# Two layers of memory-segment attention and ReLU blocks: banks of five and three turned slots, moved input moments and mask, an ordered ReLU, memory tokens by VectorE

## The chip, the core and the metric

The kernel runs on one core of a Trainium2 chip. TensorE (PE) multiplies, VectorE (DVE) and ScalarE (ACT) read its results out of PSUM and do the elementwise work, GpSimd (POOL) does elementwise work in SBUF, and SyncE (SP) issues most of the DMAs. The metric is the time of one execution on the device, in microseconds (us); 1589.74 is the median of three runs of the kernel before.

## The reference

Two identical layers; a layer is a recurrent attention over segments and a ReLU block, each behind a layer norm and added to its input (x has 2048 rows of 512).

```python
def _A_ref(x, mem0, Wq, Wk, Wv, Wo, seg_len):     # H=32, Dh=128, M=8, seg_len=32
    mask = (idx[:, None] < M) | (idx[:, None] >= idx[None, :])
    mem = mem0
    for s in range(n_seg):                        # 64 segments, one after the other
        h = jnp.concatenate([mem, xs], axis=1)    # 8 memory tokens and 32 rows
        q, k, v = (einsum('btd,dhe->bhte', h, W) for W in (Wq, Wk, Wv))
        scores = jnp.where(mask, (q @ k.T) * scale, -1e9)
        p = _softmax(scores, axis=-1)
        o = einsum('bhte,hed->btd', p @ v, Wo)
        mem = o[:, :M, :]                         # the next segment's memory
        outs.append(o[:, M:, :])
def _B_ref(x, w1, w2):                            # Dff=1376
    return maximum(x @ w1, 0) @ w2
x = x + _A_ref(_layernorm(x), ...); x = x + _B_ref(_layernorm(x), ...)   # twice
```

The memory of segment s comes out of segment s-1, so that the 64 segments of a layer are a chain.

## The kernel before

The kernel walks through 68 steps k = 0 to 67. A step handles segment k of the first layer (a = 0) and segment k-4 of the second (a = 1), each where it exists, so that steps 4 to 63 have both ("dual" here) and the first four and last four have one ("single"). L = 40 tokens a segment; tokens of both layers lie side by side in HT as 80 columns, so one weight load of Wq or Wk serves both.

A dual step, in TensorE's order: half 0 of the heads (queries and keys in batches of 6, 6 and 4 heads, `qk`, L592, matmuls on L578), a piece of the deferred output projection of the step before (`block`, L364), scores of half 0 (L612), queries and keys of half 1, the dense block's first product (`dense_h`, L495), scores of half 1, more of the output projection, the dense block's second product (`dense_y`, L520, first 18 matmuls of it), the transposes of half 1's probabilities (`transpose_p`, L652), the last 4 matmuls of `dense_y`, the weighted values (`weighted_v`, L670, matmuls on L685), the memory tokens' output (`output_mem`, L616), values of the second layer (`values1`), the turning of the new memory (`new_memory`, L817, tile mt), and the memory's values (`memory_values`, L759, matmuls on L768). Then the next step's queries begin.

Who does what beside that:

- Query results are evicted from PSUM by ScalarE (L584), key results by VectorE (L586). They share the pool ps_c of three banks, so the third query batch takes the bank of the first key batch. ps_c also holds the tiles that probabilities are turned through, mt and the memory's values.
- The score banks `sp_tiles` are filled with the mask by VectorE (`masks`, L602) before the scores are added into them. For half 0 this is done in `normalize_step` at the end of the step before; for half 1 inside `qk(1, ...)`, one mask behind the second key eviction and one behind the third.
- Softmax: maximum (L628) and subtraction (L632) on VectorE, exponential on ScalarE (L634), sum and reciprocal on VectorE (L644, L645), multiplication (L649) on POOL, but on VectorE for the last layer of half 1. Half 0's probabilities are turned by a transposing DMA (`turn_p`, L666). Half 1's are turned by TensorE in two PSUM tiles of four slots (a slot is two heads), one evicted by ScalarE and one by VectorE (L663).
- The dense block's first product is evicted with a ReLU by ScalarE (L518), in two pieces.
- `new_memory` writes the new memory tokens from mt into HT (for queries and keys, VectorE, L841) and into HTm (for the memory's values, ScalarE, L838).
- Input rows come in blocks of 128. A block is loaded (`load_xb`, at k%4 = 0), gets its moments (`moments_x`, L230) in step k%4 = 1, is normalized (L227) at the end of step k%4 = 2, and is turned by a transposing DMA (`inputs_T`) in step k%4 = 3. There are blocks to do for k = 2 and for dual steps up to k = 47.
- In k = 5, 9, ..., 49 the values of three further groups of input heads are computed (`values_at`, `split`). These steps are called light here, after the name in the code; in them `dense_h` is emitted in two pieces, the second behind half 1's scores and softmax, and ScalarE copies the values to vst (L311).

The queues of PE, DVE, SP and POOL take the instructions in the order in which the program emits them (`manual_schedule`); ScalarE's order is made by the framework's planner. `high_priority` marks blocks for that planner. `tc.issue_after(ins)` puts the instructions of its block behind `ins` on their engine.

Of the kernel before, what the change touches and what calls it, by code (L numbers as in the profile page):

```python
# [8 lines left out]
F32 = mybir.dt.float32  # L9
ALU = mybir.AluOpType  # L10
ACTF = mybir.ActivationFunctionType
# [11 lines left out]
def kernel(  # L23
# [14 lines left out]
    nc = tc.nc  # L38
    _, S, Dm = A_x.shape
    _, H, Dh = A_Wq.shape[0], A_Wq.shape[1], A_Wq.shape[2]  # L40
    M = A_mem0.shape[1]
# [3 lines left out]
    L = M + SEG  # L45
# [7 lines left out]
    SCALE = float(Dh) ** -0.5  # L53
# [6 lines left out]
    ps_c = ctx.enter_context(tc.tile_pool(name="ps_c", bufs=3, space=PSUM))  # L60
# [41 lines left out]
    xbs = {}  # L102
# [84 lines left out]
    HT = const.tile([128, NC4, 2, L], BF)  # L187
# [8 lines left out]
    P_sb = const.tile([128, 8, 128], BF)  # L196
    nc.gpsimd.memset(P_sb[:], 0.0)
    P1_sb = const.tile([128, 16 * L + 24], BF)
    nc.gpsimd.memset(P1_sb[:], 0.0)
    PT_sb = const.tile([128, 8, 2, L], BF)  # L200
    PT0 = const.tile([128, 8, 128], BF)
# [15 lines left out]
    def stat_tail(stats, of=""):  # L217
        mom = wk.tile([128, 3], F32, tag="ln_mv" + of, bufs=2 - len(of), name="mv")
        mv, rstd = mom[:, 0:2], mom[:, 2:3]
        nc.vector.bn_aggr(out=mv, in_=stats[:])  # L220
        nc.vector.tensor_scalar_add(out=rstd, in0=mv[:, 1:2], scalar1=LN_EPS)  # L221
        nc.gpsimd.tensor_tensor(out=rstd, in0=rstd, in1=mhalf_t[:], op=ALU.pow)  # L222
        return mv, rstd

    def normalize(eng, dst, src, mom, lo, hi):
        mv, rstd = mom
        eng.tensor_scalar(out=dst[lo:hi, :], in0=src[lo:hi, :], scalar1=mv[lo:hi, 0:1], scalar2=rstd[lo:hi, 0:1],  # L227
                          op0=ALU.subtract, op1=ALU.mult)

    def moments_x(n):  # L230
        stats = wk.tile([128, 6], F32, tag="ln_stats", bufs=1)
        nc.vector.bn_stats(out=stats[:], in_=xbs[n][:])
        return stat_tail(stats, "x")

    def transpose_pe(xn):
        tp = ps_fill.tile([128, NC4, 128], BF, tag="fill", name="tpx")
# [255 lines left out]

    def dense_h(d, parts=slice(None)):  # L495
        if not 0 <= d <= LAST:
            return
        lo, hi = span(d)
        n = hi - lo

        def cols(c4):
            return xnT_tiles[d + 2][:, c4, lo:hi]

        if not parts.start:
            hT_tiles[d] = wk.tile([128, NFC, 64], BF, tag="hT", bufs=1, name="hT")
        hT = hT_tiles[d]
        pieces = ((8, NFC), (0, 4), (4, 8)) if d == LAST - 1 else ((8, NFC), (0, 8))
        for f0, f1 in pieces[parts]:
            hp = ps_fill.tile([128, 8, 64], F32, tag="fill", name="hp")
            for fc in range(f0, f1):  # L510
                u = F_LAST + 128 * fc if fc < NFC - 1 else 0
                for c4 in range(NC4):
                    nc.tensor.matmul(hp[:, fc - f0, 0:n], lhsT=w1_sb[:, c4, u:u + 128],  # L513
                                     rhs=cols(c4), start=(c4 == 0), stop=(c4 == NC4 - 1))
            if (f0, f1) == (4, 8):
                nc.vector.tensor_scalar_max(out=hT[:, f0:f1, 0:n], in0=hp[:, 0:f1 - f0, 0:n], scalar1=0.0)
            else:
                nc.scalar.activation(out=hT[:, f0:f1, 0:n], in_=hp[:, 0:f1 - f0, 0:n], func=ACTF.Relu)  # L518

# [72 lines left out]
    def qk(hf, act, between=None, behind=None):  # L592
        res = []
        for n, (o, nh) in enumerate(BATCHES):
            res.append((o, nh) + tuple(qk_batch(n, 16 * hf + o, nh, act[0], act[-1] + 1, None if n else between)))
            if n == 0 and behind:
                behind()
            if hf and n > 0:
                masks(*act[n - 1:n])
        return res  # L600

    def masks(*act):  # L602
        for a in act:
            nc.vector.tensor_copy(out=sp_tiles[a], in_=maskb2)  # L604
# [11 lines left out]
    def output_mem(k, wo, h0=0, h1=H):  # L616
        n, c = divmod(k % 4, 2)
        for h in range(h0, h1):
            j = h % 4
            nc.tensor.matmul(wo[32 * j:32 * j + 32, :], lhsT=OTm[:, h, n, 2 * M * c:2 * M * c + 4 * M], rhs=Wo_sb[:, h, :],  # L620
                             start=(h < 4), stop=(h >= H - 4), tile_position=(0, 32 * j))

    def exponentials(act):
        mxs, ess = {}, {}
        for a in act:
            sp = sp_tiles[a]
            mxs[a] = wk.tile([128, 8], F32, tag="mx", bufs=2, name="mx")
            nc.vector.tensor_reduce(out=mxs[a][:], in_=sp, axis=AX.X, op=ALU.max)  # L628
        for a in act:
            sp = sp_tiles[a]  # L630
            es = ess[a] = wk.tile([128, 8, L], F32, tag="es", bufs=2, name="es")
            nc.vector.tensor_tensor(out=es[:], in0=sp, in1=mxs[a][:].unsqueeze(2).to_broadcast([128, 8, L]),  # L632
                                    op=ALU.subtract)
            nc.scalar.activation(out=es[:], in_=es[:], func=ACTF.Exp, scale=SCALE)  # L634
        return ess

    def softmax(hf, act, by_pe=False, ess=None):
# [11 lines left out]
            eng.tensor_tensor(out=P, in0=es[:],  # L649
                              in1=sm[:].unsqueeze(2).to_broadcast([128, 8, L]), op=ALU.mult)  # L650

    def transpose_p(hf):  # L652
        for p, copy in ((0, nc.scalar.copy), (1, nc.vector.tensor_copy)):
            tp = ps_c.tile([128, 4, 2, L], F32, tag="c", name="tp")
            for sl in range(4):
                for a in range(2):
                    c = L * (2 * (4 * p + sl) + a)
                    P = P1_sb[:, c:c + 64] if hf else P_sb[:, 4 * p + sl, 64 * a:64 * a + 64]
                    nc.tensor.matmul(tp[64 * a:64 * a + 64, sl], lhsT=P, rhs=ident_q,  # L659
                                     start=True, stop=True, tile_position=(0, 64 * a))  # L660
            PT = PT_sb[:, 4 * p:4 * p + 4] if hf else \
                PT0[:, 4 * p:4 * p + 4].rearrange("p s (g q) -> p s g q", g=2)[:, :, :, 0:L]
            copy(out=PT, in_=tp[:])  # L663

    def turn_p():
# [151 lines left out]
    def new_memory(k, cont, wo):  # L817
        wm_sb = wm_tiles[k] = wk.tile([128, Dm], BF, tag="vst", bufs=5, name="wm")
        nc.scalar.copy(out=wm_sb[:], in_=wo[:])
        values1(k + 1, 0)  # L820
        if k == 2:
            values0(*values_at(k)[0])
        c = 1 - k % 2
        mt = ps_c.tile([128, NC4, 2, M], F32, tag="c", name="mt")
        for c4 in range(NC4):
            for r in range(0, 128, 32):
                nc.tensor.matmul(mt[r:r + 32, c4].rearrange("p a m -> p (a m)"),  # L827
                                 lhsT=wm_sb[:, c4 * 128 + r:c4 * 128 + r + 32],
                                 rhs=sel[:, 4 * M * c:4 * M * c + 2 * M], start=True, stop=True,
                                 tile_position=(0, r))  # L830
        lo, hi = cont[0], cont[-1] + 1

        single = len(layers(k)) == 1
        by_act = k == 0 or has1(k + 1)

        def to_values():
            copy = nc.scalar.copy if by_act else nc.vector.tensor_copy
            copy(out=HTm[:, :, lo * M:hi * M], in_=mt[:, :, lo:hi, :].rearrange("p c a m -> p c (a m)"))  # L838

        def to_queries():  # L840
            nc.vector.tensor_copy(out=HT[:, :, lo:hi, 0:M], in_=mt[:, :, lo:hi, :])  # L841

        for f in (to_values, to_queries) if single else (to_queries, to_values):
            f()

    def prepare(k):
        if k <= LAST:
# [54 lines left out]
    def step(k):  # L902
        act = layers(k)
        single = len(act) == 1
        cont = [a for a in act if k - DELTA * a + 1 < NSEG]
        n_x = k // 4 + 4
        has_x = n_x < NXT
# [4 lines left out]
        with tc.high_priority(offset=PRIO):  # L912
            behind = norm_rows.pop(k, None)
            if k == 1:
                def behind():
                    normalize(nc.vector, xbs[3], xbs[3], moments_x(3), 0, 128)
            qks = qk(0, act, behind=behind)
            load_values(k, act)
            if k == 1:
                memory_values(k)  # L920
                inputs_T(3)
# [5 lines left out]
        with tc.high_priority(offset=PRIO):  # L927
            transpose_step(k)
            load_memory_values(k, act)
            scores(qks, act)  # L930
            ess = exponentials(act)

        def probabilities():

# [22 lines left out]
        if single:  # L957
            dense_h(k - 2, slice(0, 1) if k == LAST else slice(None))
            block(k, mid, H)
            if k == LAST:  # L960
                keep_busy(3)
        elif light:
            dense_h(k - 2, slice(1, None))
            block(k, 16, H)
        else:
            block(k, part, H)
# [4 lines left out]
            add_output(k - 1)  # L971
        if k == LAST:
            add_last(k - 1, 0)
        if (k % 4 == 1 and k > 1 or k == 2) and has_x:
            mom["x"] = moments_x(n_x)
        with tc.high_priority(offset=PRIO):
            transpose_p(1)
        if ahead and k < LAST:
            dense_y(k - 2, f_mid, NFC)
        tokens_in(k + 1)  # L980
# [35 lines left out]
                memory_values(k + 1)  # L1016
        with tc.high_priority(offset=PRIO):
            prepare(k + 1)
        if k % 4 == 2 and has_x:
            normalize(nc.vector, xbs[n_x], xbs[n_x], mom["x"], 0, 128)  # L1020

    mom = {}
    with tc.manual_schedule(engines={mybir.EngineType.PE, mybir.EngineType.DVE, mybir.EngineType.SP,
                                   mybir.EngineType.Pool}):
        load_rest()
        tp = transpose_pe(mem0)
# [80 lines left out]
```

## Time and profile before

| what | us |
|---|---|
| median of 3 runs (1589.31 to 1591.1) | 1589.74 |
| the profiled execution | 1592.04 |
| its span, first to last instruction | 1590.3 |
| step k = 20 (k%4 = 0), from 483.24 to 506.49 | 23.25 |
| step k = 21 (light), to 529.27 | 22.78 |
| step k = 22 (k%4 = 2), to 552.49 | 23.22 |
| step k = 23 (k%4 = 3), to 575.85 | 23.36 |
| step k = 51 (k%4 = 3, no input block left), from 1201.17 to 1224.30 | 23.13 |

A step is counted from its first query matmul to that of the next step. A timeline line has the start, the duration (of a merged group, from its first start to its last end), engine, line, operation, output <- inputs, shape, how many instructions it merges, and in brackets the engine's idle time before it and what ended that. A matmul's record lasts about 0.2 us while the next one starts 0.002 to 0.2 us behind it, so a merged PE line ends 0.2 after the next group has begun, and short pauses show in starts alone. The granted clock of TensorE is 0.999 of full speed.

### The profile page before, as it was taken

To read this page: it belongs to the slowest core of one execution; us is meant where nothing else is said; L and a number is where in the kernel's file an instruction comes from. 1 tells how busy PE (TensorE), PEld (TensorE's weight loads), DVE (VectorE), ACT (ScalarE), POOL (GpSimd) and SP (SyncE) were. 2 spreads that over 40 slices of the span, in tenths; PEclk is the share of its full clock that TensorE was granted. 3 is DMA by queue.
4 is the path that set the end of the run, shared out by engine and by line. 5 is a ranking of instruction groups with operands and counts; after the bars stand their busy time and mean duration, and the time that the engine had idled before them with its cause. 6 is when DMAs were issued, how large, how long until landed. Compare 5 with 4: busy or idle time off the path is not lost.

```text
span 1590.3 us, 95168 instructions
## 1 busy us (share of the span) xinstructions
PE 1560.3 (98%) x42866; PEld 1292.3 (81%) x42866; DVE 1297.9 (82%) x3300; ACT 734.5 (46%) x1732; POOL 350.1 (22%) x670
## 2 busy tenths in 40 slices
PE   5999999999999999999999999999999999999998
PEld 3677888888898888889888888988888788788876
DVE  4578888888888888888888888888888888888876
ACT  3435445444544545454454545445444544545432
POOL 2012222222222222222222222222222222222110
PEclk9999999999999999999999999999999999999999
DMA  9733433344343344434334443443343334334321
GB/s 368 244 81 78 78 83 89 70 98 82 72 87 83 80 79 98 82 75 84 83 87 71 99 83 75 84 83 89 67 98 78 73 84 80 82 73 94 75 69 40
DMA packets 222022, 146.27 MB, mean 92 GB/s; under 512 B 123464, under 2 KB 215984, under 8 KB 221616
## 3 DMA queue, kind: packets, MB, share of 16 engines
q1 hardware_dynamic: 218448, 135.96, 38.1%
q8 instruction: 336, 5.51, 1.6%
q0 software_dynamic: 3072, 4.20, 1.1%
q14 instruction: 70, 0.57, 0.1%
q10 hardware_dynamic: 96, 0.03, 0.0%
HBM read 65.41 MB, written 45.35 MB: 70 GB/s over the span
## 4 chain that ended last, share of the span: by engine, by line
PE 96%; DMA 2%; DVE 1%; SPq 1%; issue 0%; ACT 0%; POOL 0%; POOLq 0%
PE qp L578 38%; PE wox L364 10%; PE wo L620 8%; PE vm L768 7%; PE v L345 7%; PE hp L513 5%; PE sp L531 5%; PE pv L685 4%; PE sp L612 4%; PE vp L305 3%; DMA Wv_sb<-in_A_Wv_dram 2%; PE tp L659 1%; PE wox L387 1%; SPq L134 1%; PE mt L827 0%
## 5 line engine op out<-in xcount | busy, mean ns | idle before, releaser
L584 ACT CAST QT<-qp 128x480 bf16<-128x480 f32 (+3 forms) x408 | 201.5, 494 | 398.9 <-PE qp L578 398.7
L578 PE MATMUL qp<-HT,Wq_sb 128*128 128x80 bf16 (+1 forms) x8704 | 371.5, 200 | 3.3 <-POOL HT L757 1.2
L578 PE MATMUL qp<-HT,Wk_sb 128*128 128x80 bf16 (+1 forms) x8704 | 369.3, 199 | 1.9 <-issue 1.5
L578 PEld LDWEIGHTS <-Wq_sb 128*128 128x128 bf16 x8704 | 326.6, 100 | 36.4 <-issue 29.3
L578 PEld LDWEIGHTS <-Wk_sb 128*128 128x128 bf16 x8704 | 328.2, 100 | 3.2 <-issue 2.4
L586 DVE CAST KT<-qp 128x480 bf16<-128x480 f32 (+3 forms) x408 | 232.0, 569 | 97.2 <-PE qp L578 90.2
L649 POOL TENSOR_TENSOR P_sb<-es,sm 128x320 bf16<-128x320 f32 x185 | 130.8, 721 | 721.3 <-ACT es L634 419.9
L364 PE MATMUL wox<-Wo_sb,OTx 128*64 128x256 bf16 x2880 | 173.6, 273 | 0.0
L628 DVE TENSOR_REDUCE mx<-sp 128x8 f32<-128x320 f32 x256 | 114.9, 487 | 67.8 <-PE sp L612 66.3
L364 PEld LDWEIGHTS <-OTx 128*64 128x64 bf16 x2880 | 150.2, 110 | 2.9
L634 ACT ACTIVATE es<-es 128x320 f32<-128x320 f32 x256 | 110.3, 468 | 61.2 <-DVE es L632 60.4
L768 PE MATMUL vm<-Wv_sb,HTm 128*32 128x512 bf16 x2176 | 130.4, 380 | 0.8 <-DVE HT L841 0.8
L644 DVE TENSOR_REDUCE sm<-es 128x8 f32<-128x320 f32 x256 | 118.2, 462 | 15.1 <-ACT es L634 4.8
L345 PE MATMUL v<-Wv_sb,xnT 128*32 128x512 bf16 x2048 | 128.7, 378 | 0.0
L620 PE MATMUL wo<-Wo_sb,OTm 128*32 128x512 bf16 x2144 | 128.6, 380 | 0.0
L604 DVE CAST sp<-maskb 128x320 f32<-128x320 bf16 x256 | 118.4, 484 | 0.0
L632 DVE TENSOR_TENSOR es<-sp,mx 128x320 f32<-128x320 f32 x256 | 113.7, 483 | 1.6
L531 PE MATMUL sp<-w_sb,hT 128*64 128x256 bf16 (+4 forms) x1452 | 104.5, 277 | 0.0
L772 ACT CAST VmS<-vm 128x512 bf16<-128x512 f32 x134 | 78.5, 586 | 46.7 <-PE vm L768 46.7
L513 PE MATMUL hp<-xnT,w_sb 128*128 128x64 bf16 (+1 forms) x2948 | 98.8, 192 | 0.4 <-DVE xnT L436 0.4
L222 POOL TENSOR_TENSOR mv<-mv,mhalf_t 128x1 f32<-128x1 f32 x82 | 45.9, 559 | 233.6 <-DVE mv L221 233.6
L768 PEld LDWEIGHTS <-HTm 128*32 128x32 bf16 x2176 | 58.6, 96 | 47.1 <-issue 2.6
(122 smaller groups left out, 2089.3 us busy)
## 6 DMA issues: line engine op xcount, KB each, us to landing
Vs<-vd SPq DMA_DIRECT2D x96, 256.0 KB
vd<-vst SPq DMA_DIRECT2D x181, 128.0 KB
vmd<-VmS SPq DMA_DIRECT2D x134, 128.0 KB
Vs<-vmd SPq DMA_DIRECT2D x254, 32.0 KB
Vs<-vmd SPq DMA_DIRECT2D x60, 128.0 KB
Wq_sb<-in_A_Wq_dram SPq DMA_DIRECT2D x2, 2048.0 KB
Wk_sb<-in_A_Wk_dram SPq DMA_DIRECT2D x2, 2048.0 KB
Wv_sb<-in_A_Wv_dram SPq DMA_DIRECT2D x2, 2048.0 KB
```

Source lines behind the costliest of these rows:

```text
L345: nc.tensor.matmul(vp[32 * j:32 * j + 32, :], lhsT=tokens[:, c4, :], rhs=Wv_sb[:, c4, n * 512:(n + 1) * 512], start=(c4 == 0), stop=(c4 == ...
L364: nc.tensor.matmul(out[64 * j:64 * j + nr, 0:256], lhsT=lhsT, rhs=rhs[:, 256 * j:256 * j + 256], start=start, stop=stop, tile_position=(0, ...
L513: nc.tensor.matmul(hp[:, fc - f0, 0:n], lhsT=w1_sb[:, c4, u:u + 128], rhs=cols(c4), start=(c4 == 0), stop=(c4 == NC4 - 1))
L531: nc.tensor.matmul(sp_banks[bank][64 * j:64 * j + n, 0:w], lhsT=hT_tiles[d][0:fs, fc, 0:n], rhs=w2_flat[0:fs, fc * Dm + 256 * j:fc * Dm + ...
L578: nc.tensor.matmul(qp[:, hi, 0:ncol], lhsT=W_sb[:, c4, h * Dh:(h + 1) * Dh], rhs=HT[:, c4, a_lo:a_hi, :], start=(c4 == 0), stop=(c4 == NC4 ...
L584: nc.scalar.copy(out=dst[:, 0:nh, a_lo * L:a_hi * L], in_=qp[:, 0:nh, 0:ncol])
L586: nc.vector.tensor_copy(out=dst[:, 0:nh, a_lo * L:a_hi * L], in_=qp[:, 0:nh, 0:ncol])
L604: nc.vector.tensor_copy(out=sp_tiles[a], in_=maskb2)
L620: nc.tensor.matmul(wo[32 * j:32 * j + 32, :], lhsT=OTm[:, h, n, 2 * M * c:2 * M * c + 4 * M], rhs=Wo_sb[:, h, :], start=(h < 4), stop=(h > ...
L644: nc.vector.tensor_reduce(out=sm[:], in_=es[:], axis=AX.X, op=ALU.add)
L649: eng.tensor_tensor(out=P, in0=es[:], in1=sm[:].unsqueeze(2).to_broadcast([128, 8, L]), op=ALU.mult)
L768: nc.tensor.matmul(vp[32 * j:32 * j + 32, :], lhsT=HTm[:, c4, :], rhs=Wv_sb[:, c4, n * 512:(n + 1) * 512], start=(c4 == 0), stop=(c4 == NC ...
```

## The change

1. `transpose_p` takes a size for its first bank. In dual steps the tile of half 1 that ScalarE evicts has five slots and VectorE's three; single steps keep four and four.
2. The moments of an input block in dual light steps are split: bn_stats goes behind the first key eviction of the step's half 0, the rest stays where it was. The normalization goes from the end of step k%4 = 2 to behind the first key eviction of half 0 in step k%4 = 3. Step k = 2 keeps the old order.
3. In dual steps the mask of the first layer for half 1 is written behind half 0's subtractions, and not behind the second key eviction of half 1.
4. In light steps the second ReLU of `dense_h` is put behind the last exponential of half 1 on ScalarE.
5. In dual steps `new_memory` writes HTm first, by VectorE, and then HT, by ScalarE.

```diff
-    def moments_x(n):
+    def stats_x(n):
         stats = wk.tile([128, 6], F32, tag="ln_stats", bufs=1)
         nc.vector.bn_stats(out=stats[:], in_=xbs[n][:])
-        return stat_tail(stats, "x")
+        return stats
+
+    def moments_x(n):
+        return stat_tail(stats_x(n), "x")
...
-    def dense_h(d, parts=slice(None)):
+    def dense_h(d, parts=slice(None), behind_exp=False):
...
+            elif behind_exp:
+                with tc.issue_after(last_exp[0].ins):
+                    nc.scalar.activation(out=hT[:, f0:f1, 0:n], in_=hp[:, 0:f1 - f0, 0:n], func=ACTF.Relu)
...
-            if hf and n > 0:
+            if hf and n > 0 and (n == 2 or len(act) == 1):
                 masks(*act[n - 1:n])
...
-            nc.scalar.activation(out=es[:], in_=es[:], func=ACTF.Exp, scale=SCALE)
+            last_exp[0] = nc.scalar.activation(out=es[:], in_=es[:], func=ACTF.Exp, scale=SCALE)
...
-    def transpose_p(hf):
-        for p, copy in ((0, nc.scalar.copy), (1, nc.vector.tensor_copy)):
-            tp = ps_c.tile([128, 4, 2, L], F32, tag="c", name="tp")
-            for sl in range(4):
+    def transpose_p(hf, cut=4):
+
+        for s0, ns, copy in ((0, cut, nc.scalar.copy), (cut, 8 - cut, nc.vector.tensor_copy)):
+            tp = ps_c.tile([128, ns, 2, L], F32, tag="c", name="tp")
+            for sl in range(ns):
...
         def to_values():
-            copy = nc.scalar.copy if by_act else nc.vector.tensor_copy
+            copy = nc.scalar.copy if by_act and single else nc.vector.tensor_copy
...
         def to_queries():
-            nc.vector.tensor_copy(out=HT[:, :, lo:hi, 0:M], in_=mt[:, :, lo:hi, :])
-
-        for f in (to_values, to_queries) if single else (to_queries, to_values):
-            f()
+            copy = nc.vector.tensor_copy if single else nc.scalar.copy
+            copy(out=HT[:, :, lo:hi, 0:M], in_=mt[:, :, lo:hi, :])
+
+        to_values()
+        to_queries()
...
+            if not single and k % 4 == 1 and has_x:
+                def behind():
+                    mom["stats"] = stats_x(n_x)
+            if not single and k % 4 == 3 and has_x:
+                def behind():
+                    normalize(nc.vector, xbs[n_x], xbs[n_x], mom["x"], 0, 128)
             qks = qk(0, act, behind=behind)
...
             ess = exponentials(act)
+            if not single:
+                masks(act[0])
...
-            dense_h(k - 2, slice(1, None))
+            dense_h(k - 2, slice(1, None), True)
...
-        if (k % 4 == 1 and k > 1 or k == 2) and has_x:
+        if k == 2 and has_x:
             mom["x"] = moments_x(n_x)
+        elif not single and k % 4 == 1 and has_x:
+            mom["x"] = stat_tail(mom["stats"], "x")
         with tc.high_priority(offset=PRIO):
-            transpose_p(1)
+            transpose_p(1, 4 if single else 5)
...
-        if k % 4 == 2 and has_x:
+        if k == 2 and has_x:
             normalize(nc.vector, xbs[n_x], xbs[n_x], mom["x"], 0, 128)
```

More of the change, by code (lines that the diff above doesn't have):

```diff
@@ L621, in output_mem @@
                              start=(h < 4), stop=(h >= H - 4), tile_position=(0, 32 * j))
+    last_exp = [None]
     def exponentials(act):
@@ L650, in softmax @@
                               in1=sm[:].unsqueeze(2).to_broadcast([128, 8, L]), op=ALU.mult)
-    def transpose_p(hf):
-        for p, copy in ((0, nc.scalar.copy), (1, nc.vector.tensor_copy)):
-            tp = ps_c.tile([128, 4, 2, L], F32, tag="c", name="tp")
-            for sl in range(4):
+    def transpose_p(hf, cut=4):
+        for s0, ns, copy in ((0, cut, nc.scalar.copy), (cut, 8 - cut, nc.vector.tensor_copy)):
+            tp = ps_c.tile([128, ns, 2, L], F32, tag="c", name="tp")
+            for sl in range(ns):
                 for a in range(2):
-                    c = L * (2 * (4 * p + sl) + a)
-                    P = P1_sb[:, c:c + 64] if hf else P_sb[:, 4 * p + sl, 64 * a:64 * a + 64]
+                    c = L * (2 * (s0 + sl) + a)
+                    P = P1_sb[:, c:c + 64] if hf else P_sb[:, s0 + sl, 64 * a:64 * a + 64]
                     nc.tensor.matmul(tp[64 * a:64 * a + 64, sl], lhsT=P, rhs=ident_q,
                                      start=True, stop=True, tile_position=(0, 64 * a))
-            PT = PT_sb[:, 4 * p:4 * p + 4] if hf else \
-                PT0[:, 4 * p:4 * p + 4].rearrange("p s (g q) -> p s g q", g=2)[:, :, :, 0:L]
+            PT = PT_sb[:, s0:s0 + ns] if hf else \
+                PT0[:, s0:s0 + ns].rearrange("p s (g q) -> p s g q", g=2)[:, :, :, 0:L]
             copy(out=PT, in_=tp[:])
```

## The prediction

> **What bounds the kernel.** I read the busy table and the chain of waits first, then the timelines of single steps, one engine at a time.
>
> ```profile
> PE 1560.3 (98%) x42866; PEld 1292.3 (81%) x42866; DVE 1297.9 (82%) x3300; ACT 734.5 (46%) x1732; POOL 350.1 (22%) x670
> ...
> PE 96%; DMA 2%; DVE 1%; SPq 1%; issue 0%; ACT 0%; POOL 0%; POOLq 0%
> ```
>
> TensorE has work in nearly every nanosecond and is 96% of the chain. The change neither adds nor removes a matmul (the 16 transposing matmuls of half 1 are only cut 10 and 6), so it can gain only the pauses between matmuls that another engine causes. These are short: a batch's matmuls start 0.036 us apart, a matmul's record lasts 0.2 us, and a pause of 0.1 us is seen only as a late start. The sums go by starts, over the 60 steps with both layers (k = 4 to 63). A step lasts 23.2 us. Three kinds of pause belong to what is changed.
>
> The first stands at the head of every step with k%4 = 3. In TensorE's timeline, step 23 (from 552.49) and step 51 (from 1201.17), which has no input rows left to normalize:
>
> ```profile
> 555.08 1.03 PE L578 MATMUL qp<-HT,Wk_sb 128*128 128x80 bf16 x24
> 556.11 0.74 PE L578 MATMUL qp<-HT,Wq_sb 128*128 128x80 bf16 x16
> ...
> 1203.76 1.03 PE L578 MATMUL qp<-HT,Wk_sb 128*128 128x80 bf16 x24
> 1204.62 0.74 PE L578 MATMUL qp<-HT,Wq_sb 128*128 128x80 bf16 x16
> ```
>
> From the second key batch to the third query batch it is 1.03 us in step 23 and 0.86 in step 51. That query batch takes the PSUM bank that the first key eviction (L586) empties. VectorE in step 23, then in step 51:
>
> ```profile
> 554.98 0.40 DVE L227 TENSOR_SCALAR xb<-xb,mv 128x512 bf16<-128x512 bf16 x1
> 555.40 1.40 DVE L586 CAST KT<-qp 128x480 bf16<-128x480 f32 x2
> ...
> 1203.76 0.66 DVE L586 CAST KT<-qp 128x480 bf16<-128x480 f32 x1
> 1204.82 0.66 DVE L586 CAST KT<-qp 128x480 bf16<-128x480 f32 x1 [0.41 <-PE qp L578]
> ```
>
> The input's normalization, last on VectorE in the step before, pushes the eviction from 2.59 us into the step (1203.76 - 1201.17) to 2.91.
>
> The second pause lies inside the weighted values. Step 22:
>
> ```profile
> 546.13 0.49 DVE L663 CAST PT_sb<-tp 128x320 bf16<-128x320 f32 x1
> ...
> 546.59 0.18 PE L685 MATMUL sp<-PT_sb,Vs 40*128 40x40 bf16 x1
> 546.68 0.37 PE L685 MATMUL pv<-PT_sb,Vs 40*128 40x40 bf16 x16
> ```
>
> The last 16 products start 0.09 us after their predecessor, where 0.02 is usual: head 24 needs VectorE's half of the turned probabilities, which ends at 546.62. It comes so in 14 of the steps with k%4 = 2, 14 with k%4 = 0 and 11 with k%4 = 1.
>
> The third is in the light steps (k = 5 to 49, k%4 = 1). ScalarE, VectorE and TensorE of step 21:
>
> ```profile
> 519.40 0.47 ACT L634 ACTIVATE es<-es 128x320 f32<-128x320 f32 x1 [0.93 <-DVE es L632]
> 519.78 0.58 ACT L518 ACTIVATE hT<-hp 128x512 bf16<-128x512 f32 x1
> 520.26 0.46 ACT L634 ACTIVATE es<-es 128x320 f32<-128x320 f32 x1
> ...
> 521.51 0.49 DVE L649 TENSOR_TENSOR P_sb<-es,sm 128x320 bf16<-128x320 f32 x1
> 521.92 0.69 DVE L232 BATCH_NORM_STATS2 stats<-xb 128x6 f32<-128x512 bf16 x1
> ...
> 522.15 0.48 PE L659 MATMUL tp<-ident,P_sb 128*64 128x80 bf16 x16
> ...
> 522.93 0.48 DVE L663 CAST PT_sb<-tp 128x320 bf16<-128x320 f32 x1
> ```
>
> The ReLU gets between the exponentials, the second probabilities end at 522.00, and the transposes start 0.15 later. The last dense matmul before them had started at 521.93; in steps 20 and 22 this distance is 0.11, here 0.22.
>
> **Part by part.**
>
> *Normalization of the input, from the end of step k%4 = 2 to behind the first key eviction of k%4 = 3* (k = 7 to 47, 11 times). The eviction goes back to 2.59 and the pause of 0.17 goes: 11 x 0.17 = 1.87 us gained. In its new place it has step 51's idle 0.41 before the second key eviction, and lasts 0.40: free. Without that cover the second key eviction would slip, which costs nothing until its bank is asked for by half 1 at 5.75 us, 1.4 us after its end (4.31). Its transposing DMA stands on SP behind the probabilities' one (issued about 11 us into the step), so nothing on SP waits longer; POOL's queue is not passed.
>
> *Moments of the input, to behind the first key eviction of the light step* (11 times). 0.69 us, where step 21 has 0.42 idle: the second key eviction is 0.2 to 0.3 late and ends near 4.6, against scores from 5.15 that follow the third key batch (evicted from 4.80, when TensorE is done). Free, and off VectorE at 521.92, where it delays PT_sb. The aggregate (0.18), the add (0.15) and POOL's power (0.56) stay.
>
> *ReLU behind the exponentials* (12 light steps). The second exponential starts about 519.80 (pairs elsewhere are 0.4 apart). In full steps the last probabilities start 1.35 after the first sum (544.59 after 543.24): 521.26 instead of 521.51. They will overlap POOL's own multiplication (520.81 to 521.52) by 0.26, as in step 20 (498.56 for 0.63, POOL's until 498.83), and then take 0.63, not 0.49: end 521.89, transposes 522.04, which is where TensorE is ready (521.93 + 0.11). Gain 0.11 x 11, and 0.22 at k = 49, where the start was 0.22 late: 1.43 us. The ReLU itself would start at 520.2 and end near 520.8; dense_y needs it at 521.02. Slack about 0.15; price below.
>
> *Banks of five and three.* ScalarE's copy grows from 320 to 400 columns: 0.43 for 320 and 0.56 for 480 give 0.49, plus 0.035 for two more transposes. In step 22 it ends at 546.26 (now 546.16), and its first use is at 546.41, with some 0.06 for the signal: 0.09 to spare. VectorE's copy shrinks to 240 columns, 0.41 by the key eviction of that shape, and is needed two heads (0.05 us) later. The pause of 0.07 goes. In k%4 = 2: 14 x 0.07 = 0.98 us. In light steps: 11 x 0.07 = 0.77. In k%4 = 0 nothing: there the next matmul (wo, L620) starts 0.05 us after ScalarE's second copy of the first result, and that does not move.
>
> *Mask for half 1 beside the keys.* VectorE writes it (0.40 start to start) after the subtractions of half 0, where it idles 0.21 (step 20) to 0.80 before the next key eviction. Worst case that eviction, the sums and POOL's probabilities are 0.2 late in k%4 = 0; the transposing DMA of those has its last 256-byte packet done 13.7 us into step 22, and its first use at 16.7, and the third key eviction waits for TensorE anyway. Zero, both ways; at the worst 15 x 0.1.
>
> *Memory tokens.* VectorE writes HTm first, ScalarE HT, with the durations swapped (0.22 each). ScalarE does its copy in HTm's place:
>
> ```profile
> 527.07 0.22 ACT L838 CAST HTm<-mt 128x64 bf16<-128x64 f32 x1
> 527.61 0.59 ACT L349 CAST vst<-v 128x512 bf16<-128x512 f32 x1 [0.32 <-ACT HTm L838]
> 528.57 0.59 ACT L772 CAST VmS<-vm 128x512 bf16<-128x512 f32 x1 [0.38 <-PE vm L768]
> ```
>
> HT is then there at 527.3 and needed at 529.27; HTm comes 0.3 sooner. I find only scattered waits for HTm (0.06 at k = 57): 0 to 0.2 gained, taken as 0. Behind the first VmS it would end at 528.57 + 0.59 + 0.22 = 529.38 and cost about 0.15 a step.
>
> **Sum.** 1.87 + 1.43 + 0.98 + 0.77 = 5.05 us. The profiled execution took 1592.04 (span 1590.3 and 1.74 around it): it would take 1587.0. It is 2.3 above the median shown, so the same sum on the median gives 1589.74 - 5.05 = 1584.7. TensorE also has pauses that no semaphore explains (0.70 us idle at 374.25, ended by "issue", and others of 0.2 to 0.5, some 5 us in all); where they fall can change with the code, and I allow 1.5 us each way for them.
>
> **Rivals.** No measurement of this kernel tells less than 0.2%, 3.2 us, from no change.
>
> *(a) As summed*, 1583.0 to 1586.5. For it: the stalls and the steps without them stand side by side in the trace. Chance 0.57.
>
> *(a') The two multiplications exclude each other.* If VectorE's probabilities wait until POOL's are through, they end at 521.52 + 0.49 = 522.01 as before, the 1.43 falls away, and 3.62 or 1586.1 is left. Against it: in step 20 this would give an end at 499.32, and the row ends at 499.19. Chance 0.06. The Trainium skill (SBUF — State Buffer, "Who interferes with whom") states such an exclusion, for a whole instruction, between a VectorE instruction with two SBUF inputs and a GpSimd one that reads SBUF; this trace shows 0.14 lost where it would have 0.27.
>
> *(b) The gains are given back.* Only the head of step 3 is gained (1.87, so 1587.9), because something else holds the light step's transposes and PT_sb: ScalarE's longer copy, or the ReLU. ScalarE's order is planned, not written out; if it takes the first vst copy (0.58, due within 0.3 us of the ReLU) before it, the ReLU ends about 521.5, dense_y starts at 521.6 instead of 521.03 and the transposes are 0.48 later than now: 12 x 0.48 = 5.8 lost against 1.87 + 0.98 + 0.77 = 3.6, so 1591.9. For it: slacks of 0.09 and 0.15 are thin. Against: hp is done 0.4 us before that vp, and the rows give both slacks. Chance 0.20.
>
> *(c) Slower: HT comes late from ScalarE.* In every step the query matmuls of the next one wait for it, at 529.27 in step 21; with 0.06 for the signal the copy must start by 528.99. From 0.08 us later (60 x 0.084 = 5.05) the whole sum is gone. If ScalarE takes it behind the first VmS, 60 x 0.15 = 9 us are lost and 1593.7 results. For it: four other copies stand there within 2.8 us, in a planned order, and before the change VectorE wrote HT alone. Against: HTm stood in the same place, and mt is ready 1.3 us before that VmS can start. Chance 0.12.
>
> *(d) Nothing happens*, because the order that results is the old one: 1589.7. Chance 0.05.
>
> **Numbers.** Predicted 1584.7. (b) and (d) set the upper end: 1590.0 leaves out (c) and the late ReLU; the lower end, 1582.8, is the sum with 0.2 for HTm and 1.5 of luck. Faster by over 0.2% (under 1586.6): (a), (a') and a little of (b), 0.66. Slower by over 0.2% (over 1592.9): (c), 0.12. Within 0.2%: the rest, 0.22.
>
> **What would show it.** In the new profile: the first key eviction of k%4 = 3 at 2.59 us, not 2.91, third query batch 0.86 after the second key batch; the ReLU after both exponentials and done 0.15 before dense_y; transposes 0.11 after the last dense matmul; 0.02 before the last 16 products; HT on ScalarE between the two value copies. Steps: 23.13 for k%4 = 3, 22.61 for the light ones, 23.15 for k%4 = 2, unchanged for k%4 = 0. I am wrong if TensorE waits for hT, HT or ScalarE's PT_sb, or if pauses of the unexplained sort grow.

## The result, and the profile after

The changed kernel takes 1582.49 us (median of six runs, 1580.01 to 1583.93) against 1590.52 (six runs) before: a ratio of 0.9949, 95% interval 0.9936 to 0.9962, 8.1 us saved. The forecast was 1584.7, with 5.05 saved; the measured time lies 0.3 us below the range. The direction was right, and so were the three kinds of pause for which the forecast counted a gain; the memory tokens, a fourth, it took as 0.

Profiled, the span went from 1590.3 to 1580.5 us. Step times from the two traces; each is the shortest among the steps of its kind, so that pauses scattered over single steps do not enter:

| steps | before | after | forecast |
|---|---|---|---|
| k%4 = 0 (k = 8 to 56) | 23.240 | 23.191 | unchanged |
| light (k = 9 to 45) | 22.787 | 22.533 | 22.61 |
| k%4 = 2 (k = 10 to 58) | 23.213 | 23.079 | 23.15 |
| k%4 = 3 (k = 7 to 47) | 23.300 | 23.078 | 23.13 |

Every kind of step is 0.05 to 0.08 us shorter than forecast. From before to after, the differences of the table, taken over all two-layer steps, make up about 8.2 of the 9.8 us between the two spans; the rest lies in scattered pauses and in the first and last steps. The busy line of the page after, engine by engine:

```profile
PE 1549.4 (98%) x42865; PEld 1284.3 (81%) x42866; DVE 1288.5 (82%) x3300; ACT 739.2 (47%) x1732; POOL 349.2 (22%) x670
```

TensorE has the same matmuls (one record fewer in the trace) and is as full as before; the span shrank by pauses alone. The head of step 23 (from 548.80) in the timeline after, TensorE:

```profile
551.39 1.03 PE L584 MATMUL qp<-HT,Wk_sb 128*128 128x80 bf16 x24
552.25 0.74 PE L584 MATMUL qp<-HT,Wq_sb 128*128 128x80 bf16 x16
```

and VectorE:

```profile
551.44 0.66 DVE L592 CAST KT<-qp 128x480 bf16<-128x480 f32 x1
552.01 0.41 DVE L227 TENSOR_SCALAR xb<-xb,mv 128x512 bf16<-128x512 bf16 x1
552.45 0.66 DVE L592 CAST KT<-qp 128x480 bf16<-128x480 f32 x1
```

The third query batch starts 0.86 us behind the second key batch, where it was 1.03: the pause is gone, and the normalization fills the idle time between two key evictions without delaying the second, which starts 3.65 us into the step as in step 51 before. (The first key eviction starts 2.64 us into the step, not at the 2.59 forecast, because the step itself begins 0.05 us sooner.) The weighted values of step 22, VectorE and TensorE:

```profile
542.57 0.41 DVE L672 CAST PT_sb<-tp 128x240 bf16<-128x240 f32 x1
...
543.03 0.18 PE L694 MATMUL sp<-PT_sb,Vs 40*128 40x40 bf16 x1
543.05 0.36 PE L694 MATMUL pv<-PT_sb,Vs 40*128 40x40 bf16 x16
```

The last 16 products start 0.02 us behind the product before them, where it was 0.09. The light step 21, ScalarE, VectorE and TensorE:

```profile
516.10 0.87 ACT L642 ACTIVATE es<-es 128x320 f32<-128x320 f32 x2 [0.93 <-DVE es L640]
516.88 0.58 ACT L522 ACTIVATE hT<-hp 128x512 bf16<-128x512 f32 x1
...
517.95 0.62 DVE L657 TENSOR_TENSOR P_sb<-es,sm 128x320 bf16<-128x320 f32 x1
...
518.73 0.47 PE L668 MATMUL tp<-ident,P_sb 128*64 128x80 bf16 x16
...
519.25 0.41 DVE L672 CAST PT_sb<-tp 128x240 bf16<-128x240 f32 x1 [0.40 <-PE tp L668]
```

The two exponentials stand together, the ReLU behind them; VectorE's multiplication takes 0.62 (forecast 0.63), and the transposes start 0.106 us behind the last dense matmul (0.218 before). VectorE now waits 0.40 for TensorE before it copies PT_sb; before it was the other way round.

What the forecast had at nothing is the start of the memory's value matmuls (vm), here in step 22 before the change:

```profile
550.29 0.22 ACT L838 CAST HTm<-mt 128x64 bf16<-128x64 f32 x1
...
550.55 0.23 PE L479 MATMUL xp<-wm,sel 128*32 128x128 bf16 x4
550.62 0.15 PEld L768 LDWEIGHTS <-HTm 128*32 128x32 bf16 x8
550.65 0.40 PE L768 MATMUL vm<-Wv_sb,HTm 128*32 128x512 bf16 x4
```

and after it:

```profile
546.33 0.23 DVE L847 CAST HTm<-mt 128x64 bf16<-128x64 f32 x1 [0.54 <-PE mt L836]
...
546.91 0.23 PE L482 MATMUL xp<-wm,sel 128*32 128x128 bf16 x4
546.91 0.38 PEld L777 LDWEIGHTS <-HTm 128*32 128x32 bf16 x12
546.97 0.60 PE L777 MATMUL vm<-Wv_sb,HTm 128*32 128x512 bf16 x8
```

From the first matmul of the group before (xp) to the first vm it is 0.10 us before and 0.06 after. From the last xp it is 0.085 and 0.046, and the 32 vm starts lie 0.01 closer together: 0.05 us a step, and the same in all dual steps up to k = 58.

### The profile page after: what moved, and what is told of

Read it like the earlier page. It is cut to its first block, busy times and chain, and to the rows that moved or that the text cites. A ratio compares the mean times of both kernels' runs of the same rounds, so it can differ in the third digit from the quotient of the medians.

```text
span 1580.5 us, 95107 instructions
## 1 busy us (share of the span) xinstructions
PE 1549.4 (98%) x42865; PEld 1284.3 (81%) x42866; DVE 1288.5 (82%) x3300; ACT 739.2 (47%) x1732; POOL 349.2 (22%) x670
## 5 line engine op out<-in xcount | busy, mean ns | idle before, releaser
L777 PEld LDWEIGHTS <-HTm 128*32 128x32 bf16 x2176 | 54.9, 97 | 47.8 <-issue 2.5
```

What stands on the lines that cost most here:

```text
L777: nc.tensor.matmul(vp[32 * j:32 * j + 32, :], lhsT=HTm[:, c4, :], rhs=Wv_sb[:, c4, n * 512:(n + 1) * 512], start=(c4 == 0), stop=(c4 == NC ...
```

## The experiments

The first five take one part of the change each, put into the kernel before. The interval of each ratio reaches 1.3 us and more to either side, as much as most parts are worth; what a part does is therefore read from the step times and starts in its trace, and the ratio only has to agree.

**The memory tokens alone.**

```diff
-            copy = nc.scalar.copy if by_act else nc.vector.tensor_copy
+            copy = nc.scalar.copy if by_act and single else nc.vector.tensor_copy
...
-            nc.vector.tensor_copy(out=HT[:, :, lo:hi, 0:M], in_=mt[:, :, lo:hi, :])
+            copy = nc.vector.tensor_copy if single else nc.scalar.copy
+            copy(out=HT[:, :, lo:hi, 0:M], in_=mt[:, :, lo:hi, :])
...
-        for f in (to_values, to_queries) if single else (to_queries, to_values):
-            f()
+        to_values()
+        to_queries()
```

> The kernel before with the memory-token part of the change alone. Theory (the prediction missed a wait of the memory's value matmuls for HTm): the first of them comes 0.046 us after the matmul before it instead of 0.085, the 32 of them are 0.01 shorter, each of the 55 dual steps k = 4 to 58 is 0.05 us shorter, the whole about 2.7 us faster than before. Rival (the 3 us beyond the forecast are fewer unexplained pauses of TensorE, by luck or by where the code lies): steps as before, time within 1 us of before.

Measured: ratio 0.9989 (0.9980 to 0.9998), 1.7 us saved. The first vm comes 0.046 us after its predecessor, and k%4 = 0, light and k%4 = 2 steps are 0.05 us shorter (23.189, 22.735, 23.161). The theory holds, with one exception: k%4 = 3 stays at 23.299. TensorE at the head of step 23 of this kernel:

```profile
555.03 1.03 PE L578 MATMUL qp<-HT,Wk_sb 128*128 128x80 bf16 x24
556.12 0.73 PE L578 MATMUL qp<-HT,Wq_sb 128*128 128x80 bf16 x16
```

1.09 us instead of 1.03. The step begins 0.05 us earlier, but VectorE's first key eviction does not: it starts 26.12 us behind the start of the step before, where it was 26.13. So TensorE gives the 0.05 back there. In the changed kernel, without the normalization ahead of that eviction, it keeps them.

**The banks of five and three alone.**

```diff
-            transpose_p(1)
+            transpose_p(1, 4 if single else 5)
```

(with the new `transpose_p`).

> The kernel before with banks of five and three alone. Theory: the pause of 0.07 before the last 16 weighted-value matmuls goes in k%4 = 0, 1 and 2; steps k%4 = 2 and light ones are 0.085 us shorter (14 and 11 of them: 2.1 us), k%4 = 0 unchanged because the output matmuls still wait for ScalarE's copies. Rival (ScalarE's longer copy is what the weighted values then wait for): head 16 comes later than now, steps not shorter.

Measured: ratio 0.9991 (0.9983 to 1.0), 1.4 us. The distance before the last 16 products is 0.022 in all kinds of step, where it was 0.091 in most steps with k%4 = 0 and 2 and in the light ones; light steps 22.700 and k%4 = 2 23.130, 0.085 shorter each, k%4 = 0 23.240 as before. The pause was there in ten light steps (k = 9 to 45), not in eleven. The theory holds; ScalarE's longer copy holds nothing up.

**The moments and the normalization alone.**

```diff
+            if not single and k % 4 == 1 and has_x:
+                def behind():
+                    mom["stats"] = stats_x(n_x)
+            if not single and k % 4 == 3 and has_x:
+                def behind():
+                    normalize(nc.vector, xbs[n_x], xbs[n_x], mom["x"], 0, 128)
...
-        if k % 4 == 2 and has_x:
+        if k == 2 and has_x:
```

(with `stats_x` and the second half of the moments as in the whole change).

> The kernel before with moments and normalization of the input moved, nothing else. Theory: 11 steps k%4 = 3 are 0.17 us shorter (head of the step), 11 light steps 0.085 (PT_sb on VectorE in time): 2.8 us in all. Rival (the moved instructions delay the second key eviction so that TensorE waits for its bank or for the scores): a later start of half 1's queries in the light steps, less than 1 us gained.

Measured: ratio 0.9981 (0.9972 to 0.9990), 3.0 us. k%4 = 3 goes from 23.300 to 23.133, light steps from 22.787 to 22.700. The theory holds. In the light steps it removes the same 0.085 as the banks do; in the changed kernel it counts once.

**The ReLU alone.**

```diff
+                with tc.issue_after(last_exp[0].ins):
+                    nc.scalar.activation(out=hT[:, f0:f1, 0:n], in_=hp[:, 0:f1 - f0, 0:n], func=ACTF.Relu)
```

(in the light steps' second call of `dense_h`).

> The kernel before with the ReLU of the light steps put behind the last exponential, nothing else. Theory: transposes of the 12 light steps 0.11 us earlier (0.22 in k = 49), the pause before the last 16 weighted-value matmuls stays at 0.07; 1.5 us in all. Rival (VectorE's and GpSimd's multiplications exclude each other, or the ReLU is late for dense_y): light steps as before or longer.

Measured: ratio 0.9991 (0.9982 to 1.0), 1.4 us. Light steps 22.667 (0.12 shorter), k = 49 22.588 (0.235 shorter); transposes 0.106 us after the last dense matmul, the pause before the last products still 0.09. The theory holds, for VectorE's and GpSimd's multiplications too.

**The mask alone.**

```diff
-            if hf and n > 0:
+            if hf and n > 0 and (n == 2 or len(act) == 1):
...
+            if not single:
+                masks(act[0])
```

> The kernel before with the first mask of half 1 moved to behind the subtractions of half 0, nothing else. Theory: no step changes by more than 0.01 us; the key eviction behind it is 0.1 later in k%4 = 0 and nothing waits for it. Rival (the mask was in the way of the scores of half 1): shorter light steps.

Measured: ratio 0.9997 (0.9985 to 1.0008). All four kinds of step within 0.008 us of before. In the kernel before, this part neither gains nor costs anything.

The next two ask why 0.05 us were to be had at vm.

**The spare columns of HTm by ScalarE, in the kernel before.** HTm has two writers: ScalarE puts the new tokens in, GpSimd 16 spare columns of later input rows.

```diff
-            nc.gpsimd.tensor_copy(out=HTm[:, :, 2 * M:32], in_=spare_T(k + 1))
+            nc.scalar.copy(out=HTm[:, :, 2 * M:32], in_=spare_T(k + 1))
```

> The kernel before, with the spare columns of HTm (the 16 that new memory does not fill) copied by ScalarE instead of GpSimd; HT stays on VectorE and HTm's tokens on ScalarE. Theory (the wait for HTm costs 0.05 because the first weight load has two writers to wait for, ScalarE and GpSimd, and the second wait is an instruction of its own on TensorE that runs only once ScalarE's signal is there): with one writer that instruction is gone, the first value matmul comes 0.046 after its predecessor though HTm is as late as before, steps 0.05 shorter in k = 4 to 58, time 2 to 3 us below before. Rival (mere lateness of ScalarE's copy): 0.085 and 23.24 us in k%4 = 0 stay.

Measured: ratio 0.9980 (0.9971 to 0.9990), 3.1 us; k%4 = 0 23.194, light 22.739, k%4 = 2 23.162, so 0.05 less, as with the exchange of the copies. Its step 22:

```profile
549.17 0.22 ACT L838 CAST HTm<-mt 128x64 bf16<-128x64 f32 x1
...
549.44 0.23 PE L479 MATMUL xp<-wm,sel 128*32 128x128 bf16 x4
549.44 0.38 PEld L768 LDWEIGHTS <-HTm 128*32 128x32 bf16 x12
549.50 0.60 PE L768 MATMUL vm<-Wv_sb,HTm 128*32 128x512 bf16 x8
```

HTm ends 0.05 us ahead of the first xp matmul (549.39 against 549.44), as late as before the change (550.51 against 550.55), and yet the weights are loaded at once and vm comes after 0.06. What differs is in the view of the line of vm, sequencer instructions, before:

```profile
L768 PEldq EVENT_SEMAPHORE  x61: 51/51/747, 69.2 to 1560.3; - x61
```

and in this kernel:

```profile
L768 PEldq EVENT_SEMAPHORE  x4: 51/51/51, 108.6 to 1556.3; - x4
```

(number; shortest, median and longest duration in ns). With two writers the first weight load has two semaphores to wait for, and one of the waits is an instruction of 0.051 us in TensorE's queue. Before the change it is the wait for ScalarE. In step 22 HTm ends at 550.505; the instruction runs from 550.542 to 550.593, so that it ends 0.03 us after the last xp matmul has started, and the weight load follows at 550.618. In the changed kernel the instruction is still there:

```profile
L777 PEldq EVENT_SEMAPHORE  x61: 51/51/747, 68.8 to 1551.7; - x61
```

But it waits for VectorE, whose copy ended 0.37 us before the last xp matmul, and is through 0.07 us before it. So it is neither the lateness alone nor the extra instruction alone, but the extra instruction behind a late signal.

**Both copies by VectorE, HT first, in the kernel before.**

```diff
-            copy = nc.scalar.copy if by_act else nc.vector.tensor_copy
+            copy = nc.scalar.copy if by_act and single else nc.vector.tensor_copy
```

> The kernel before, with both memory-token copies on VectorE, HT first and HTm behind it. HTm is then some 0.15 us earlier than before and 0.2 later than in the changed kernel, and GpSimd still writes the spare columns. Theory (a wait instruction costs nothing where the signal is there when it is reached): steps 0.05 shorter as with the whole exchange. Rival (it needs HTm as early as the change makes it): less or nothing; and if the longer VectorE row counts, the first key eviction is 0.14 later and the third query batch pauses.

Measured: ratio 0.9992 (0.9982 to 1.0001). HTm ends 0.24 us before the last xp matmul, the wait instruction is there, vm comes after 0.047: a signal 0.2 us earlier than before is enough, as the theory says. k%4 = 0 is 0.043 shorter. But k%4 = 3 is 0.08 longer (23.381), since the first key eviction starts 0.13 later in the step: the second half of the rival's expectation came true as well, and most of the gain is gone. So it matters that ScalarE takes the HT copy.

**The changed kernel without the token part.**

```diff
-            copy = nc.scalar.copy if by_act and single else nc.vector.tensor_copy
+            copy = nc.scalar.copy if by_act else nc.vector.tensor_copy
...
+        for f in (to_values, to_queries) if single else (to_queries, to_values):
+            f()
```

> The changed kernel with the memory-token part undone. Theory: 0.05 us more in each of the dual steps to k = 58, 2.7 us slower than the changed kernel, the other gains stay (k%4 = 0 as before the change, 23.24; light 22.58; k%4 = 2 and 3 near 23.13). Rival (the gains of the parts overlap): other steps change as well.

Measured: ratio to before 0.9969 (0.9954 to 0.9985), against 0.9949 for the whole change: 5.0 us saved, not 8.1. Steps 23.244, 22.586, 23.133 and 23.131. This kernel has every part for which the forecast counted a gain, and it takes about the time that was forecast for the whole (5.05 saved). The two intervals overlap a little; that the tokens make the difference is shown by the steps, each kind of which is 0.05 us longer than in the changed kernel.

**A further edit on the changed kernel.** In k%4 = 0 the output matmuls (wo) still wait for ScalarE's second copy of the first weighted values. VectorE gets that copy and ScalarE the second layer's tokens instead. The changed kernel ran beside it.

```diff
-            swap = ride0(k) and t == 0
+            swap = ride0(k) and t == 0 and not (a == 0 and lo == M or a == 1 and lo == 0)
```

> The changed kernel once more, beside the next one on the same chip. Expected: 8 us below before, within 1.5.

> The changed kernel; in the steps k%4 = 0 VectorE copies the first 16 rows' share of the first weighted values (the instruction that the output matmuls wait for) and ScalarE the second layer's memory tokens instead. Theory (there the output matmuls wait 0.11 us for ScalarE's second copy): ScalarE's and VectorE's copies end together near 17.60 us into the step instead of 17.68, the output matmuls start 0.05 to 0.1 earlier, 15 steps, about 1 us faster than the changed kernel. Rival (VectorE is late there itself, or the step is then held by the eviction of the output): no change in k%4 = 0.

Measured: the changed kernel 0.9952 (0.9940 to 0.9965), this one 0.9972 (0.9961 to 0.9984). k%4 = 0 takes 23.448, 0.257 more. Its copies in step 20:

```profile
498.48 0.38 ACT L712 CAST OTm<-pv 128x96 bf16<-128x96 f32 x2 [0.23 <-PE pv L694]
498.75 1.58 DVE L712 CAST OTm<-pv 128x192 bf16<-128x192 f32 x6 [0.22 <-ACT OTm L712]
...
499.25 1.05 PE L626 MATMUL wo<-Wo_sb,OTm 128*32 128x512 bf16 x16 [0.30 <-DVE OTm L712]
```

and in the changed kernel:

```profile
497.21 0.68 ACT L712 CAST OTm<-pv 128x96 bf16<-128x96 f32 x3 [0.23 <-PE pv L694]
497.24 1.58 DVE L712 CAST OTm<-pv 128x96 bf16<-128x96 f32 x6
...
497.72 1.26 PE L626 MATMUL wo<-Wo_sb,OTm 128*32 128x512 bf16 x18
```

VectorE waits for ScalarE (0.22, ended by ScalarE's copy) where the two ran side by side. Both now read the same PSUM tile, and the program puts a wait between them; that the shared tile is the reason was not tested by itself. Neither theory nor rival had that. Run again, the changed kernel saved 7.6 us by its ratio, as expected; it is the fastest here.

## Why the prediction was right and wrong

- *Head of step k%4 = 3*, 11 x 0.17 = 1.87: the start of the third query batch moved by 0.17. Right.
- *Light steps' transposes*, 1.43: 11 x 0.12 + 0.235 = 1.56. Right, by the mechanism named: both exponentials together, 0.62 for the overlapped multiplication (0.49 without overlap), the ReLU in time. Rivals (a') and (b) fell with it.
- *Banks*, 0.07 in 25 steps = 1.75: 0.083 to 0.087 each, in 24 steps, 2.0. Right in its mechanism, a little small in its size. The count was off by one: in the trace of before, the pause stands in ten steps with k%4 = 1 (k = 9 to 45; 0.02 at k = 5 and 49), where the prediction read eleven. k%4 = 0 gained nothing from them, as forecast.
- *Mask*, 0: right.
- *Memory tokens*, "0 to 0.2 gained, taken as 0": wrong, and the step that failed. It is 0.05 us in each of 55 steps, 2.7 us, nearly the whole of the 3.0 that were missing. ScalarE took HT in time, as argued against rival (c). But the prediction listed only the waits for HTm that stand out (0.06 at k = 57) and passed over the 0.085 us ahead of vm. That distance stands in every two-layer step up to k = 58, and starts stand as far apart at other changes from one kind of matmul to another (0.106 before the scores and before the output matmuls in step 22), so that it is easily taken for the price of such a change. The trace of before had the counter-example: in the last dual steps no spare columns are left to write. Step 60 before the change:

```profile
1432.81 0.22 ACT L838 CAST HTm<-mt 128x64 bf16<-128x64 f32 x1
...
1433.08 0.23 PE L479 MATMUL xp<-wm,sel 128*32 128x128 bf16 x4
1433.08 0.38 PEld L768 LDWEIGHTS <-HTm 128*32 128x32 bf16 x12
1433.13 0.61 PE L768 MATMUL vm<-Wv_sb,HTm 128*32 128x512 bf16 x8
```

There vm comes 0.05 us behind xp's first matmul, not 0.10, with the same ScalarE copy just as late, and step 60 lasts 23.195 where other steps of its kind take 23.240.

- *The range* stopped at 1582.8, because the unknown of this term was bounded by the few waits I had listed (0.2) and not by the 60 pauses of up to 0.085 that stand there (at most 5 us).

The terms as measured, 1.87 + 1.56 + 2.0 + 2.7 = 8.1, agree with the 8.1 of the runs (5.5 without the tokens, where 5.05 were forecast). The parts taken alone save 1.7 + 1.4 + 3.0 + 1.4 = 7.5 by their ratios, with well over a microsecond of uncertainty in each; they overlap in the light steps (0.085 counted twice) and help each other in k%4 = 3 (0.05 that the tokens alone give back).

## What to carry to other kernels

A pause that is the same in every step is not thereby a property of the hardware: look for a step that lacks one of its inputs and compare. Where an operand has writers on two engines, its first reader may need a wait instruction of its own; let the engine that finishes first write the part that is read first, or let one engine write all of it. On a full engine, look at starts, not at listed waits: 8 us here were pauses of 0.05 to 0.24 us, and of these the table of waits shows next to nothing (for the weighted values, one wait of 0.2 us).

## What was not expected of the hardware

TensorE also pauses where no semaphore explains it, most often within the query and key batches, and the places change from run to run. In each of the profiles above, the two-layer steps that are longer than the shortest of their kind add up to 1.7 to 5.9 us in this way. In three traces (before, the change, and the change without tokens), 34 of the 35 such pauses of over 0.1 us in these steps ended 1.0 to 1.7 us after the end of a packet on the instruction queue, which has one packet every 4.7 us or so. That points to instruction loading; it is a match in time alone, and was not tried.
